# A routing step handed out earlier, and the last group of a gated layer in another order

## The chip, the core and the metric

The program runs on one core of one Trainium2 chip. The core has five engines with instruction streams of their own: TensorE (PE, matmuls and transposes through the array; its weight loads are listed as PEld), VectorE (DVE), ScalarE (ACT), GpSimd (POOL) and SyncE (SP, which only issues DMAs and loads of registers). They wait for each other by semaphores. The metric is the time of one execution on the device, in microseconds; less is better. For before, the median of three runs is 842.74 us (839.76 to 843.46).

## The reference

Three layers follow each other on 2304 tokens of 512 numbers, all in float32:

```python
# 1: attention over a feature map, 4 batches x 8 heads x 576 positions
phi(x) = concat(exp(p), exp(-p)),  p = x @ w_phi - max|x @ w_phi|
attn   = (phi(q) @ (phi(k)^T v)) / (phi(q) @ sum phi(k))

# 2: mixture of 8 experts, each token goes to one of them
logits = x @ w_gate + modality_bias[modality_id]
e_idx  = argmax(logits);  gate_w = softmax(logits)[e_idx]
out[t] = gate_w[t] * (relu(x[t] @ w1[e_idx]) @ w2[e_idx])      # 512 -> 1024 -> 512

# 3: gated layer
result = ((x @ w_a) * (x @ w_b)) @ w_out                       # 512 -> 1536 -> 512
```

## The kernel before

Matrices are multiplied to float32 accuracy with three matmuls each: both factors are split into a high part and a remainder, and `mm3` (L53 to L56) adds high x high (L54), high x low (L55) and low x high (L56). The remainders are made by DVE (`wl` L553, `mxl` L577, `hl` L591, `gl` L829).

**Halves, tiles and steps.** The tokens are taken in two halves of 1152, each with a routing of its own (`Route`). A routing has four parts: `start` (gate and one-hot), `rank` (a matmul `rkp`, copied to `R` at L394), `place` (sorts the tokens to tiles of up to 608 tokens of one expert; writes `meta`, L464) and `table` (two matmul lookups: `tbp` gives `idx`, the tokens of each tile in order, L504; `tbq` gives the places `perm` and gates `g` of the output, L504 and L514 to L517). Its matmuls use PSUM tiles of the pool `ps_t`, which has two buffers under one tag; the transposes of the tiles use the same two.

Each half has two tiles, so there are T0, T1 (first half) and T2, T3 (second half). `Moe.run` goes through them in 8 steps a tile, step k = 8 x tile + j. Steps j = 0 to 3 are the first matrix (`l1`, 48 matmuls `hp` each), steps 4 to 7 the second (`l2`, 48 matmuls `yp` each). For the tile that comes next, the gathers (`gather`, five of them, an indirect DMA on POOL's queue by `idx`, L561, into `xg`) are asked for at j = 2, and the transposes (`transp`, five pieces of four PE transposes into `mxt`, L573, then ACT's high part `mxh` and DVE's remainder `mxl`) at j = 4 to 7. Pieces 0 to 2 hold the 304 tokens with which the first `hp` of a tile work.

**Work beside.** The dictionary `side` hands out other work at a step: the four parts of the second half's routing, `close_work` (L945 of before: the largest tile count `top` of both halves), and ten conversions of the gated layer's weights from 64-bit numbers, as they come, to float32 (`conv`, with `prep` and `narrow`: loads `raw` on SP's queue L685, ACT L689, POOL L690, DVE L691 to L698, sums L707 to L710, split L715 and L716, stores L717 and L718). All of these are handed out with a lower priority (`low`, LOWR; `conv`, LOWP).

**Who sets the order.** In this stage a scheduler sets the order of every engine's instructions before the program runs: it goes by priority and by its own estimate of when operands are ready. Each engine then runs its list strictly in order. So a part handed out at another step moves many instructions on many engines.

**The gated layer.** `Moe2.run` goes through 24 groups (token blocks of 768, each taken through 12 blocks of 128 of the 1536 hidden columns). In a group `stage` has seven input products (`PROD`, six matmuls `abp` each; a scheme with seven products in place of eight), from which ACT and DVE build the gated values `gh`, `gl`. The output products `outp(k, m)` (three matmuls `op`) add a group to six accumulators m. Before, outp of the group before stands between the input products, and the last group's six outp stand at the very end (L873 to L875). When an accumulator is complete, `finish` scales it (ACT for even m, DVE for odd) and stores it by an indirect DMA on POOL's queue (L797). PE's order is the order of the code here (`manual_schedule`).

Of the kernel before, what the change touches and what calls it, by code (L numbers as in the profile page):

```python
# [48 lines left out]
def f32(ap):  # L49
    return ap.bitcast(F32)  # L50
# [604 lines left out]
class Moe2:  # L655
# [124 lines left out]
    def run(self, ws, ts, src0, side):  # L780
        nc, n = self.nc, self.N
        seq = [(p, f) for p in range(NTOK // n // 2) for f in range(self.NF)]
        accs, gs = {}, {}

        def finish(p):
            for m, acc in enumerate(accs.pop(p)):
                bp, b = divmod(2 * p + m // 3, HALF // n)
                if m % 3 == 0:
                    os = self.p_o.tile([P, 3, DM], F32, tag="raw", name="o", bufs=2)
                o = os[:, m % 3, :]  # L790
                c = b * (n // P) + m % 3
                g2 = self.routes[bp].g2[:, c:c + 1]
                if m % 2:
                    nc.vector.tensor_scalar(out=o, in0=acc, scalar1=g2, scalar2=None, op0=ALU.mult)
                else:
                    nc.scalar.activation(o, acc, AF.Copy, scale=g2)  # L796
                st = nc.gpsimd.indirect_dma_start(  # L797
                    out=self.out[:, :],
                    out_offset=bass.IndirectOffsetOnAxis(ap=self.routes[bp].perm[:, c:c + 1], axis=0),
                    in_=o, in_offset=None)  # L800
                for other in self.stores:
                    self.tc.declare_no_dep(st.ins, other, reason="each row of the output is stored once")
                self.stores.append(st.ins)

        def outp(k, m):
            p, f = seq[k]
            if f == 0 and m == 0:
                accs[p] = [self.ps_a.tile([P, 512], F32, tag=f"a{i}", name=f"op{i}") for i in range(6)]
            gh, gl = gs[k]
            wh, wl = ws[k](1536, 512)  # L810
            ms = slice(P * (m % 3), P * (m % 3) + P)
            mm3(nc, accs[p][m], gh[:, m // 3, ms], gl[:, m // 3, ms], wh, wl, f == 0, f == self.NF - 1)
            if m == 5:
                del gs[k], ws[k]
                if f == self.NF - 1:
                    finish(p)

        def stage(k):
            p, f = seq[k]
            ct = lambda tag, shape: self.p_c.tile([P] + shape, F32, tag=tag, name=tag)  # L820
            ca, u, d = ct("ca", [2, n]), ct("u", [2, n]), ct("d", [2, n])
            out = []
            gs[k] = [self.p_g.tile([P, 2, n], F32R, tag=t, name=t) for t in ("gh", "gl")]

            def gate(i, other):
                gh, gl = (x[:, i, :] for x in gs[k])
                nc.vector.tensor_mul(ca[:, i, :], ca[:, i, :], other)  # L827
                nc.scalar.copy(gh, ca[:, i, :])  # L828
                nc.vector.tensor_sub(gl, ca[:, i, :], f32(gh))  # L829

            for i, (col, t) in enumerate(self.PROD):
                ps = self.ps_l.tile([P, 512], F32, tag="l", name="abp")[:, :n]
                wh, wl = ws[k](col, 256)
                th, tl = ts[p][t]
                for c in range(2):
                    cs = slice(P * c, P * c + P)
                    mm3(nc, ps, wh[:, cs], wl[:, cs], th[:, c, :], tl[:, c, :], c == 0, c == 1)
                x = self.p_c.tile([P, n], F32, tag="pc", name="pc", bufs=5)
                nc.scalar.copy(x, ps)  # L839
                out.append(x)  # L840
                if i == 1:
                    nc.vector.tensor_add(u[:, 0, :], x, out[0])
                elif i == 2:
                    nc.vector.tensor_add(ca[:, 0, :], x, out[0])
                elif i == 3:
                    nc.vector.tensor_add(u[:, 1, :], x, u[:, 0, :])
                elif i == 4:
                    nc.vector.tensor_add(d, u, x.unsqueeze(1).to_broadcast([P, 2, n]))  # L848
                elif i == 5:
                    nc.vector.tensor_add(x, x, u[:, 1, :])  # L850
                    gate(0, x)
                elif i == 6:
                    nc.vector.tensor_add(ca[:, 1, :], x, d[:, 0, :])
                    gate(1, d[:, 1, :])
                if k and i > 1:
                    for m in (i - 2,) if i < 6 else (4, 5):
                        outp(k - 1, m)

        src = src0
        self.rest(src, ts[0])  # L860
        for k, (p, f) in enumerate(seq):
            with self.tc.high_priority(offset=-LOWP2):
                for st in side.get(k, ()):
                    st()
            if k + 1 < len(seq) and k + 1 not in ws:
                ws[k + 1] = self.weights(k + 1)
            if f == 0 and p:
                self.rest(src, ts[p])
            with self.tc.manual_schedule(engines={mybir.EngineType.PE}):
                stage(k)  # L870
            if f == self.NF - 2 and k + 2 < len(seq):
                src, ts[p + 1] = self.terms(p + 1, self.p_s)
        with self.tc.manual_schedule(engines={mybir.EngineType.PE}):  # L873
            for m in range(6):
                outp(len(seq) - 1, m)  # L875


def low(tc, step):
# [8 lines left out]
def trn_kernel(ctx, tc, qk, v, vt, w_phi, mod_id, w_gate, bias, wm, wf, out):  # L887
# [37 lines left out]
    with ExitStack() as mctx:  # L925
        ps_t = mctx.enter_context(tc.tile_pool(name="ps_t", bufs=2, space=PSUM, **tl))
        ps_l = mctx.enter_context(tc.tile_pool(name="ps_l", bufs=3, space=PSUM, **tl))
        ypool = ctx.enter_context(tc.tile_pool(name="y", bufs=1, **tl))
        y = [ypool.tile([P, 4, YC], F32, name=f"y{i}") for i in range(2)]
        m2 = Moe2(nc, tc, wf, wsc, y, routes, out, f64)  # L930
        mo = Moe(nc, tc, mctx, cst, xs, wm, y, ps_l, ps_t)
        tiles = [(rt, t) for rt in routes for t in range(NTMIN)]
        rctx = ExitStack()
        cv = []
        nts = []
        ws = {}

        cctx = ExitStack()
        cv.append(cctx.enter_context(tc.tile_pool(name="cv", bufs=1, **tl)))

        def close_work():
            rctx.close()
            top = rpool.tile([1, 1], I32, name="top")
            n = slice(3 * NTMAX, 3 * NTMAX + 1)
            nc.vector.tensor_tensor(out=top, in0=routes[0].meta[:, n], in1=routes[1].meta[:, n], op=ALU.max)  # L945
            nts.append(nc.values_load(top[:, :], min_val=0, max_val=NTMAX))

        wk1 = rctx.enter_context(tc.tile_pool(name="rwork1", bufs=1, **tl))
        rs = routes[1].steps(wk1, ps_t, "t")
        side = {k: [low(tc, rs[f])] for f, k in enumerate((0, 3, 5, 8))}  # L950
        side[9] = [close_work]

        def conv(f):
            with tc.high_priority(offset=-LOWP):
                m2.prep(f, cv[0], 2, 2)

        K0, K1 = 3, len(tiles) * mo.NJ - 4
        for f in range(NPRE):
            side.setdefault(K0 + (K1 - K0) * f // NPRE, []).append(lambda f=f: conv(f))
        ts, src0 = {}, []  # L960

        def first():
            src, ts[0] = m2.terms(0, m2.p_s, ts.get(0), src0[0] if src0 else None)
            src0.append(src)

        def open_first():
            cctx.close()
            m2.p_t[0] = ctx.enter_context(tc.tile_pool(name="f_t", bufs=Moe2.NT0, **tl))
            m2.p_s = ctx.enter_context(tc.tile_pool(name="f_s", bufs=1, **tl))
            m2.p_w[0] = ctx.enter_context(tc.tile_pool(name="f_w0", bufs=1, **tl))  # L970
            ws[0] = m2.weights(0)
            with tc.high_priority(offset=-LOWP):
                first()

        side.setdefault(K1, []).append(open_first)
        tc.mark_branch_hint_location("extra", "LikelyTaken", engines=ENGINES)
        mo.run(tiles, side)
        with tc.If(nts[0] > NTMIN, label="extra"):
            n = slice(3 * NTMAX, 3 * NTMAX + 1)
            for rt in routes:  # L980
                extra(tc, mo, rt, nc.values_load(rt.meta[:, n], min_val=0, max_val=NTMAX))
            first()
    cv.append(ctx.enter_context(tc.tile_pool(name="cv2", bufs=1, **tl)))
    side = {}
# [65 lines left out]
```

## Time and profile before

| what | before |
|---|---|
| runs, us | 842.74, 843.46, 839.76 |
| profiled execution, us | 840.43 |
| its span, us | 838.6 |
| PE busy, us | 802.0 |
| DVE busy, us | 595.5 |
| POOL busy, us | 134.1 |

The profiled execution's span is what the profile covers; the little that lies around it makes the difference to 840.43. A row of a timeline begins with the start of an instruction in the span, then its duration, its engine, its line in the kernel and what it writes and reads. Matmuls are pipelined, so the distance of two starts, and not the duration, is what one costs. Where an engine was idle before an instruction, square brackets give the time and what ended it.

### The profile page before, as it was taken

The numbers are of one execution on the slowest core, as the hardware profiler recorded it, in microseconds if no ns is written. First come the engines' busy times: TensorE is split into PE (matmuls) and PEld (weight loads), VectorE is DVE, ScalarE is ACT, GpSimd is POOL, SyncE is SP. The second block draws the span as 40 slices with busy tenths as digits, with TensorE's granted clock in tenths as the row PEclk, the third lists the DMA queues.
The fourth block names the chain that finished last, engine by engine and source line by source line (L and its number), as shares of the span: only waits on it lengthen the run. The fifth ranks groups of instructions, "written<-read, shape, count | busy, mean of one in ns | idle before, by whom it ended". The sixth has DMA issues, their size and how long they took to land.

```text
span 838.6 us, 18331 instructions
## 1 busy us (share of the span) xinstructions
PE 802.0 (96%) x7284; PEld 752.8 (90%) x7284; DVE 595.5 (71%) x1071; ACT 375.1 (45%) x665; POOL 134.1 (16%) x164
## 2 busy tenths in 40 slices
PE   9999998899989999989899999999999999999995
PEld 7989888899989999989889899989999999999994
DVE  6877998689995989797588855675554476545553
ACT  4555555434452555444445433553333364333332
POOL 1000018433233522510031000020000002000002
PEclk9999999999998999999999999999999999999998
DMA  8755431667668888776689876576666668666631
GB/s 300 221 173 165 161 90 31 215 217 275 225 202 283 295 303 295 239 288 251 230 286 332 280 241 201 195 257 214 225 202 199 192 201 301 202 203 201 190 135 75
DMA packets 85163, 184.22 MB, mean 220 GB/s; under 512 B 27760, under 2 KB 37520, under 8 KB 85072
## 3 DMA queue, kind: packets, MB, share of 16 engines
q1 hardware_dynamic: 81872, 173.21, 61.6%
q0 software_dynamic: 3040, 9.72, 3.2%
q8 instruction: 58, 0.95, 0.5%
q14 instruction: 33, 0.27, 0.1%
q10 hardware_dynamic: 160, 0.07, 0.0%
HBM read 145.21 MB, written 37.75 MB: 218 GB/s over the span
## 4 chain that ended last, share of the span: by engine, by line
PE 24%; issue 19%; DVE 4%; POOL 2%; ACT 2%; DMA 1%; POOLq 0%; DVEq 0%; ACTq 0%
PE abp L54 5%; PE abp L56 5%; PE abp L55 5%; PE op L56 3%; PE op L55 3%; PE op L54 3%; POOL cvs L690 1%; DMA wsc<-whi 1%; POOL out L797 1%; ACT pc L839 1%; DVE gl L829 0%; DVE d L848 0%; ACT yh L744 0%; DVE ca L827 0%; DVE yl L745 0%
## 5 line engine op out<-in xcount | busy, mean ns | idle before, releaser
L839 ACT COPY pc<-abp 128x384 f32<-128x384 f32 x252 | 120.5, 479 | 199.3 <-PE abp L56 194.2
L54 PE MATMUL abp<-yh,fw 128*128 128x384 f32 x504 | 169.9, 337 | 3.2 <-ACT pc L839 2.2
L55 PE MATMUL abp<-yl,fw 128*128 128x384 f32 x504 | 169.9, 337 | 0.0
L56 PE MATMUL abp<-yh,fw 128*128 128x384 f32 x504 | 169.9, 337 | 0.0
L54 PEld LDWEIGHTS abp<-yh,fw 128*128 128x128 f32 x504 | 94.6, 188 | 13.1 <-ACT pc L839 4.0
L55 PEld LDWEIGHTS abp<-yl,fw 128*128 128x128 f32 x504 | 94.6, 188 | 7.6
L690 POOL TENSOR_SCALAR cvs<-cvs 128x768 f32<-128x768 f32 x24 | 62.7, 2612 | 210.5 <-ACT cvs L689 158.3
L56 PEld LDWEIGHTS abp<-yh,fw 128*128 128x128 f32 x504 | 94.6, 188 | 0.0
L54 PE MATMUL op<-fw,gh 128*128 128x512 f32 x216 | 85.4, 395 | 1.0 <-ACT gh L828 1.0
L56 PE MATMUL op<-fw,gl 128*128 128x512 f32 x216 | 85.3, 395 | 0.9 <-DVE gl L829 0.9
L55 PE MATMUL op<-fw,gh 128*128 128x512 f32 x216 | 85.4, 395 | 0.0
L54 PE MATMUL hp<-mxh,wh 128*128 128x304 f32 x256 | 78.8, 309 | 3.7 <-DVE hl L591 3.7
L55 PE MATMUL yp<-hl,wh 128*128 128x304 f32 x256 | 77.1, 302 | 1.0 <-DVE hl L591 1.0
L55 PE MATMUL hp<-mxl,wh 128*128 128x304 f32 x256 | 77.9, 305 | 0.0
L56 PE MATMUL yp<-hh,wl 128*128 128x304 f32 x256 | 77.7, 304 | 0.0
L56 PE MATMUL hp<-mxh,wl 128*128 128x304 f32 x256 | 77.7, 304 | 0.0
L54 PE MATMUL yp<-hh,wh 128*128 128x304 f32 x256 | 76.7, 303 | 0.5 <-ACT y L603 0.5
L797 POOL DMA_INDIRECT out<-o,perm x18 | 18.1, 1006 | 355.9 <-ACT o L796 349.4
L190 ACT ACTIVATE qts<-qtp 128x512 f32<-128x512 f32 (+1 forms) x80 | 38.3, 557 | 57.2 <-PE qtp L187 57.2
L848 DVE TENSOR_TENSOR d<-u,pc 128x768 f32<-128x768 f32 x36 | 34.4, 956 | 33.9 <-ACT pc L839 33.7
L54 PEld LDWEIGHTS hp<-mxh,wh 128*128 128x128 f32 x256 | 48.7, 191 | 4.9 <-DVE hl L591 2.8
L828 ACT CAST gh<-ca 128x384 fp32r<-128x384 f32 x72 | 36.9, 515 | 34.6 <-DVE ca L827 34.6
(191 smaller groups left out, 1584.4 us busy)
## 6 DMA issues: line engine op xcount, KB each, us to landing
fw<-wsc SPq DMA_DIRECT2D x72, 512.0 KB, 3.6
fw<-wsc SPq DMA_DIRECT2D x144, 256.0 KB, 3.3
raw<-in_moe_w SPq DMA_DIRECT2D x24, 768.0 KB, 6.2
s<-in_moe_w SPq DMA_DIRECT2D x32, 512.0 KB, 5.8
fw<-wsc SPq DMA_DIRECT2D x72, 128.0 KB, 2.6
wsc<-whi SPq DMA_DIRECT2D x12, 640.0 KB, 4.8
wsc<-wsum SPq DMA_DIRECT2D x12, 640.0 KB, 5.0
wsc<-whi SPq DMA_DIRECT2D x12, 512.0 KB, 4.2
```

The costliest lines, as they stand in the source:

```text
L54: nc.tensor.matmul(out, lh, rh, start=start, stop=False)
L55: nc.tensor.matmul(out, lh, rl, start=False, stop=False)
L56: nc.tensor.matmul(out, ll, rh, start=False, stop=stop)
L190: nc.scalar.activation(t[:, s, :n, :], ps[:, :n, :], AF.Exp, scale=1.0 - 2.0 * s)
L690: nc.gpsimd.tensor_scalar(out=s.bitcast(F32), in0=s.bitcast(F32), scalar1=LEAST, scalar2=None, op0=ALU.max)
L797: st = nc.gpsimd.indirect_dma_start(out=self.out[:, :], out_offset=bass.IndirectOffsetOnAxis(ap=self.routes[bp].perm[:, c:c + 1], axis=0), ...
L828: nc.scalar.copy(gh, ca[:, i, :])
L839: nc.scalar.copy(x, ps)
L848: nc.vector.tensor_add(d, u, x.unsqueeze(1).to_broadcast([P, 2, n]))
```

## The change

Two things. The parts of the second half's routing are handed out at steps 0, 1, 2 and 4 (all within T0) instead of 0, 3, 5 and 8. And in the last of the 24 groups of the gated layer all seven input products come first, in the order 0, 1, 2, 3, 5, 4, 6; behind them stand the output products of the group before (back 1) and of the last one (back 0), accumulator by accumulator.

```diff
-            for i, (col, t) in enumerate(self.PROD):
+            last = k + 1 == len(seq)
+            for i in (0, 1, 2, 3, 5, 4, 6) if last else range(7):
+                col, t = self.PROD[i]
...
-                if k and i > 1:
+                if k and i > 1 and not last:
                     for m in (i - 2,) if i < 6 else (4, 5):
                         outp(k - 1, m)
...
                 stage(k)
+                if k + 1 == len(seq):
+                    for back, m in ((1, 0), (1, 1), (1, 2), (0, 0), (0, 1), (0, 2), (1, 3), (0, 3), (1, 4), (0, 4), (1, 5), (0, 5)):
+                        outp(k - back, m)
...
-        with self.tc.manual_schedule(engines={mybir.EngineType.PE}):
-            for m in range(6):
-                outp(len(seq) - 1, m)
...
-        side = {k: [low(tc, rs[f])] for f, k in enumerate((0, 3, 5, 8))}
+        side = {k: [low(tc, rs[f])] for f, k in enumerate((0, 1, 2, 4))}
         side[9] = [close_work]
```

The first change moves instructions on all engines from the mixture's first steps on. On PE, in the order of before, T1's transposes stand among the `yp` of T0's last steps; these are the rows around the last of its five pieces (96 tokens wide):

```order
L54 MATMUL yp<-hh,wh 128x304
L55 MATMUL yp<-hl,wh 128x304
L573 MATMUL mxt<-ident,xg 128x96 x4
L56 MATMUL yp<-hh,wl 128x304
L54 MATMUL yp<-hh,wh 128x304 x2
L55 MATMUL yp<-hl,wh 128x304
```

Behind them T0 goes on. In the order of after, no transposes of T1 are left there: the whole five pieces stand behind the last `yp` of T0, with the second half's lookup `tbq` (`tbqr` and `lhs` are its operands, made by DVE) between them:

```order
L56 MATMUL yp<-hh,wl 128x304
L497 LDWEIGHTS lhs
L497 MATMUL tbq<-tbqr,lhs 128x45
L573 MATMUL mxt<-ident,xg 128x128 x4
...
L497 LDWEIGHTS lhs
L497 MATMUL tbq<-tbqr,lhs 128x45
L573 MATMUL mxt<-ident,xg 128x128 x12
L54 MATMUL hp<-mxh,wh 128x304 x3
L573 MATMUL mxt<-ident,xg 128x96 x4
L55 MATMUL hp<-mxl,wh 128x304
```

In the rows left out stand seven more `tbq`. In the order of before the `tbq` stand inside T1's second half of steps, directly ahead of the first transposes of T2.

On DVE, in the order of after, this stands from the last `tbqr` to the first `mxl` of T1 (`cvs`, `cvt`, `wsum` are tiles of the weight conversions, `wl` the remainder of an expert's weights):

```order
L493 TENSOR_TENSOR tbqr<-tbqh,gp 128x9x9 x3
L695 TENSOR_SCALAR cvs<-cvt 128x768
L947 TENSOR_TENSOR top<-meta_2204,meta_3445 1x1
L698 TENSOR_TENSOR wsum<-cvt,cvs 128x768
L553 TENSOR_TENSOR wl<-s,wh 128x1024
L716 TENSOR_TENSOR wsum<-wsum,whi 128x1280
L553 TENSOR_TENSOR wl<-s,wh 128x1024
L696 SCALAR_TENSOR_TENSOR cvs<-raw,cvs 128x768
L503 TENSOR_SCALAR tk<-tbq 128x9
L577 TENSOR_TENSOR mxl<-mxt,mxh 128x4x128
```

The second `mxl` comes eight rows further, the third nine rows after that, the fourth and fifth two rows after each one before. Between them stand further conversions (L691, L693, L695 to L698, L707 to L710) and the small steps of `perm` and `g`.

In the gated layer's last group, PE's rows in the order of after run on from the seven products like this (the name `op_16900` is accumulator 0; rows on an accumulator come in threes):

```order
L56 MATMUL abp<-yh,fw 128x384
L54 MATMUL op_16900<-fw,gh 128x512
L55 MATMUL op_16900<-fw,gh 128x512
L56 MATMUL op_16900<-fw,gl 128x512
L54 MATMUL op_16901<-fw,gh 128x512
...
L54 MATMUL op_16902<-fw,gh 128x512
L55 MATMUL op_16902<-fw,gh 128x512
L56 MATMUL op_16902<-fw,gl 128x512
L54 MATMUL op_16900<-fw,gh 128x512
L55 MATMUL op_16900<-fw,gh 128x512
L56 MATMUL op_16900<-fw,gl 128x512
```

The first three accumulators get the group before, then the last group, and after them come 3, 4 and 5, each with both groups one behind the other. In before, the last group's products stood between the accumulations of the group before, and accumulators 0 to 5 of the last group at the end.

## Rows read from the trace of the kernel before

**Rows 1.** The page's first part: an engine's busy time, share of span, instructions.

```profile
PE 802.0 (96%) x7284; PEld 752.8 (90%) x7284; DVE 595.5 (71%) x1071; ACT 375.1 (45%) x665; POOL 134.1 (16%) x164
```

**Rows 2.** Waits of PE, whole run: us in total, times, longest.

```profile
PE mxt L573 <- DMA xg<-xs,idx: 5.2, 1, 5.2
PE hp L54 <- DVE hl L591: 3.7, 5, 1.1
```

**Rows 3.** Busy by stretch: length, PE, PEld, DVE, ACT, POOL, clock, DMA share, GB/s.

```profile
205.00:245.00 40.00, 40.00 (x297) 39.73 (x297) 39.92 (x95) 18.72 (x29) 9.86 (x4) 1.00 0.66 220
```

**Rows 4.** Timeline of PE where T2's transposes stand: start, us, what.

```profile
247.75 0.40 PE L497 MATMUL tbq<-tbqr,lhs 128*128 128x45 bf16 x9
253.37 1.09 PE L573 MATMUL mxt<-ident,xg 128*128 128x128 f32 x4 [5.22 <-DMA xg<-xs,idx]
257.30 0.31 PE L54 MATMUL hp<-mxh,wh 128*128 128x304 f32 x1
```

**Rows 5.** Busy by stretch, the 2 us behind that wait; clock third last.

```profile
252.00:254.00 2.00, 0.63 (x3) 0.66 (x4) 2.00 (x6) 0.00 (x0) 1.59 (x2) 0.50 0.95 311
```

**Rows 6.** Timeline of PE at the end of T0 and start of T1.

```profile
215.31 0.60 PE L573 MATMUL mxt<-ident,xg 128*128 128x128 f32 x4
...
215.89 0.30 PE L55 MATMUL yp<-hl,wh 128*128 128x304 f32 x1
...
223.66 0.30 PE L54 MATMUL hp<-mxh,wh 128*128 128x304 f32 x1
...
224.91 0.30 PE L54 MATMUL hp<-mxh,wh 128*128 128x304 f32 x1
```

**Rows 7.** Timeline of DVE: an `hl`, the second routing's `R`, its last `tbqr`.

```profile
187.95 0.77 DVE L591 SCALAR_TENSOR_TENSOR hl<-hp,hh 128x608 fp32r<-128x608 f32 x1
...
205.04 0.23 DVE L394 COPY R<-rkp 128x80 f32<-128x80 f32 x1
...
244.17 0.53 DVE L493 TENSOR_TENSOR tbqr<-tbqh,gp 128x81 bf16<-128x81 bf16 x3
```

**Rows 8.** DVE by line and shape, 185 to 248: busy, mean ns, idle before.

```profile
L553 DVE TENSOR_TENSOR wl<-s,wh 128x1024 fp32r<-128x1024 f32 x9 | 11.3, 1252 | 0.0
...
L696 DVE SCALAR_TENSOR_TENSOR cvs<-raw,cvs 128x768 f32<-128x768 uint32 x6 | 5.7, 946 | 0.0
...
L691 DVE TENSOR_SCALAR cvt<-cvs 128x768 int32<-128x768 int32 x6 | 3.3, 550 | 0.3 <-POOL cvs L690 0.3
...
L716 DVE TENSOR_TENSOR wsum<-wsum,whi 128x1280 fp32r<-128x1280 f32 x2 | 3.0, 1479 | 0.0
L577 DVE TENSOR_TENSOR mxl<-mxt,mxh 128x512 fp32r<-128x512 f32 x4 | 2.7, 677 | 0.0
L716 DVE TENSOR_TENSOR wsum<-wsum,whi 128x1024 fp32r<-128x1024 f32 x2 | 2.4, 1214 | 0.0
...
L708 DVE TENSOR_TENSOR wsum<-wsum 128x256 f32<-128x256 f32 x3 | 1.2, 415 | 0.0
```

**Rows 9.** Timeline of POOL and DVE beside one conversion's maximum.

```profile
212.97 3.44 POOL L690 TENSOR_SCALAR cvs<-cvs 128x768 f32<-128x768 f32 x1 [5.15 <-ACT cvs L689]
...
213.13 0.95 DVE L696 SCALAR_TENSOR_TENSOR cvs<-raw,cvs 128x768 f32<-128x768 uint32 x1
214.00 0.42 DVE L710 TENSOR_TENSOR wsum<-wsum 128x256 f32<-128x256 f32 x1
...
214.60 1.58 DVE L553 TENSOR_TENSOR wl<-s,wh 128x1024 fp32r<-128x1024 f32 x1
```

**Rows 10.** Timeline of PE and POOL at the end of the run.

```profile
827.00 0.97 POOL L797 DMA_INDIRECT out<-o,perm  x1 [126.31 <-ACT o L796]
...
828.49 0.39 PE L55 MATMUL op<-fw,gh 128*128 128x512 f32 x1
...
828.72 0.39 PE L56 MATMUL op<-fw,gl 128*128 128x512 f32 x1
...
833.37 0.97 POOL L797 DMA_INDIRECT out<-o,perm  x1 [0.30 <-issue]
```

## The prediction

> **What bounds the kernel now.** I read the page's engine line first: PE is busy for 802.0 of 838.6 us [rows 1], so the order of PE's work is the kernel, and only what makes PE wait can be won or lost. Second the waits of PE over the run [rows 2]: 5.2 us in one piece at the transposes `mxt`, waiting for the gather `xg`, and 3.7 us in five pieces at `hp`, waiting for `hl` from DVE. Third the busy time by stretch around the second routing [rows 3]: from 205 to 245 us PE is busy for 40.00 of 40 us, and so is DVE, for 39.92, with 95 instructions. PE has no gap there only because DVE keeps just ahead of it. That is what matters most: work that DVE must do for PE there and that is put behind other DVE work costs PE time at once.
>
> Fourth PE's timeline where the third tile (T2, first of the second half) begins [rows 4]. After the last `tbq` of the second routing PE stands 5.22 us for the gather, and 4 transposes with the first 12 `hp` then take from 253.37 to 257.30, 3.93 us. In that stretch the granted clock is 0.50 [rows 5], the lower of its two levels (1.2 of 2.4 GHz), after PE had been nearly idle. At full clock the same work is taken from [rows 6]: 4 transposes and the `yp` behind them take 0.58 (215.31 to 215.89), so 0.44 for the transposes; nine `hp` take 1.25 (223.66 to 224.91), 0.139 each, so twelve 1.67. That makes 2.11, and the slow clock cost 1.82.
>
> The profiled execution took 840.43 us. The sum is made against it; the median of the three runs, 842.74, lies 2.3 higher, and the predicted time is the median plus the sum.
>
> **What the earlier routing removes.** The second half's `idx` is made in T0's last step instead of T1's third, so the gathers of T2 are issued a tile ahead of the transposes that need them: the 5.22 goes, and the 1.82 with it. -7.0. What is late next is what the rest of this text is about.
>
> **What it adds: T1's start.** In the order of before, T1's transposes stand among the last `yp` of T0, each with PE work behind it [rows 6]. In the order of after, the routing's `tbp` and `tbq` take the two PSUM buffers that the transposes share with it, and all five pieces of T1 stand behind T0's last `yp`: one `tbq`, 4 transposes, eight `tbq`, 12 transposes, then the `hp` that need them. The pieces take turns in two buffers, so a piece waits for the DVE subtraction `mxl` of an earlier one (the third for the last L516, which reads `tbq`), and the first `hp` waits for the third `mxl`. DVE's order therefore decides. Between its last `tbqr` and that third `mxl` stand 26 instructions, mostly weight conversions. With the means of [rows 8], 0.15 for each of the small ones (the 0.23 of `R` [rows 7] is the longest of these), L693 and L698 taken as L696 (same shape, two inputs), L695 as L691, L707 and L709 as L708, and 0.08 off each for overlap (213.13 + 0.95 against the next start at 214.00 [rows 9]):
> - to the first `mxl`: 0.55 + 0.946 + 1.252 + 1.479 + 1.252 + 0.946 + 0.677 and two small ones, less 0.72: 6.7
> - to the second: 0.55 + 0.946 + 0.946 + 0.415 + 0.677 and three small ones, less 0.64: 3.3
> - to the third: 0.55 + 3 x 0.415 + 2 x 0.946 + 0.677 and two small ones, less 0.72: 3.9
>
> Together 14.0 us from the last `tbqr` to the first `hp`. The fourth and fifth `mxl` are 1.7 and 0.9 later, and the 12 `hp` of the first token group cover them. PE's own work in the stretch at full clock is 0.40 for `tbq` [rows 4], 5 x 0.44 for transposes and 1.67 for 12 `hp`: 4.3. If the clock falls as in [rows 5], the twelve `hp` and the fifth piece take 3.9 behind the 14.0: 17.9, a loss of 13.6. If it doesn't fall, the loss is 14.0 less the 1.7 of `tbq` and three pieces: 12.3.
>
> To this comes PE's wait for `tbqr` itself. `R`, from the second routing's rank, stands in the order of after right behind the `hl` that began at 187.95 [rows 7], so at about 188.7 instead of 205.04. From `R` to the end of `tbqr` DVE needed 39.7 us (205.04 to 244.70), for 93 instructions that come to 39.5 by the means above; in the order of after there are 88, without the four `mxl` and one `wl`, and they come to 36.6, 2.9 less. 188.7 + 36.8: `tbqr` ends near 225.5. PE gets there at 223.66 plus 24 `yp` that still followed (3.3) less five pieces (2.2), some 224.7. Wait 0.8, between 0 and 3. The term is 13.6 + 0.8 = +14.4, from 12.3 (no clock loss, no wait) to 18 (a raw block for the conversions comes late as well).
>
> **The rest of T1.** DVE owes T1's `hl` in time: 42 instructions stand between its last `mxl` and the eighth, by the same means ([rows 8], with the 0.77 of [rows 7] for an `hl`) 30.5 us, so 47.1 from `tbqr`. PE wants it after the 17.9, 180 more `hp` (25.0), two pieces of T2 (0.9) and 21 `yp` (2.9): 46.7. +0.5, 0 to 3. The other waits for `hl`, 3.7 [rows 2], may go or grow with any shift: -1.0 taken, for DVE has four `mxl` less in T0's last steps; -3.7 to +3 as bounds.
>
> **The last gated group.** In the order of after all seven products stand first and then, for the first accumulator, the output product of the group before and of the last. Nine matmuls (accumulators 3 to 5 of the group before) no longer stand ahead of the first finished accumulator: 9 x 0.23 ([rows 10], 828.49 to 828.72) is 2.1. The six stores run on GpSimd 1.27 apart, 827.00 to 833.37, and set the end; starting 2.1 sooner, the last starts at 831.3. The last accumulator is still done in time, since the last matmul stays at 828.72, 2.6 before that. -2.1, from -1 (ACT's casts of the gate lie ahead of the first scaling) to -2.6. Order 5 before 4 costs nothing: the same seven products.
>
> Sum: +14.4 + 0.5 - 7.0 - 1.0 - 2.1 = +4.8, which is 845.2 against the profiled execution and **847.5** against the median.
>
> **Rivals.** What this measurement can tell from no change is about 0.5%, 4.2 us: 838.5 to 847.0 counts as the same.
>
> A, faster: DVE is well ahead of PE at T1's start and PE stands under 5 us. For it: `tbqr` needs only `R` and fixed work, and PE may be later than reckoned. Against: DVE would have to be 9 us earlier, and in 205 to 245 it has 0.08 us idle [rows 3]. With a stand of 2.5: 2.5 - 7.0 - 1.0 - 2.1 = -7.6, so 835.1.
>
> B, no change: T1's stand is at its low end and the waits for `hl` go: 12.3 - 7.0 - 3.7 - 2.1 = -0.5, so 842.2. For it: a PE that stands lets DVE catch up. Against: the order of DVE in T1 is as full as before.
>
> C, slower still: GpSimd's maximum L690 comes late. Its input comes by SP's queue, and in the order of after SP waits for the second half's `meta` earlier, with a weight and a raw load behind it; then DVE's L691 in the second leg waits for one L690, up to 3.44 [rows 9]. Against: in before DVE waited 0.3 for it in this whole stretch [rows 8]. 847.5 + 3.4 = 850.9.
>
> D, slower still: DVE and GpSimd shut each other out. The chain's L696 and L698 have two SBUF inputs, and GpSimd runs two L690 beside it in the order of after; DVE would stand up to 3.44 for each, 847.5 + 6.9 = 854.4. While L690 ran from 212.97 to 216.41, DVE's L696 took 0.95, its mean, and L553 1.58 against 1.252, and L690 itself was the slow one [rows 8, 9]: at most 0.33 is seen. The Trainium skill (SBUF — State Buffer, Who interferes with whom) states the strict form: a DVE instruction with two SBUF inputs contends with a GpSimd instruction that reads SBUF, and the later one blocks fully until the other ends. By that rule the time would be D's; the trace doesn't bear it out, since L696 ran inside an L690 without a loss.
>
> **How the numbers follow.** Forecast 0.45, its own range 844.5 to 851.5 (T1's term from 12.3 to 18, the others near their values), 0.30 of it above 847.0 and 0.15 below. B 0.26, all within 0.5%. A 0.13. C 0.11 and D 0.05, slower. So slower 0.46, same 0.41, faster 0.13. The range 839.5 to 854 leaves out most of A and a part of D and of late loads.
>
> **What would show it.** PE's waits after: the 5.2 for `xg` gone, and 12 to 14 us at `mxt` and `hp` for `mxl`, right after T0's last `yp`, in three pieces near 6, 3 and 4, with a granted clock of 0.50 behind them. The first store near 2 us sooner against the last product. I am wrong if PE's stand there is under 9 us, if a wait of over 3 us appears at another place, or if gathers of T2 are still waited for.

## The result, and the profile after

The changed kernel takes 850.8 us (median of six runs, 847.28 to 851.18) against 840.23 for before on the same chip: a ratio of 1.0125, 95% interval 1.0100 to 1.0151. It is slower, by 10.6 us. The forecast was slower by 4.8 (847.5 us, range 839.5 to 854): side and mechanism held, the size was less than half of what came. That the time itself lies only 3.3 above the forecast is partly luck: before's median was 842.74 when the forecast was made and is 840.23 over all six runs.

Four slips in the text ahead: the gated layer goes through 36 groups (three blocks of 768 tokens), not 24; `tbq` of before stands among T1's `hp`, not in its second half of steps; T2's gathers now begin 27 us ahead of its first transposes (227.77 and 255.07), not a whole tile; and three `hp` by L54, which need no `mxl`, stand ahead of the third `mxl`, as the rows of the order show, so the first `hp` doesn't wait for it. The first three bear on no number of the sum; by the fourth the stand was put some 0.8 us too long.

The profiled execution of after took 851.02 us with a span of 849.2. First the engine line of its page, then the waits of PE from 200 to 300 us (total, times, longest):

```profile
PE 806.3 (95%) x7283; PEld 754.6 (89%) x7284; DVE 596.8 (70%) x1071; ACT 375.9 (44%) x665; POOL 138.3 (16%) x164
```

```profile
PE mxt L573 <- issue: 5.7, 1, 5.7
PE mxt L573 <- DVE mxl L577: 5.7, 2, 4.8
PE hp L54 <- DVE hl L591: 1.2, 1, 1.2
PE yp L54 <- ACT hh L590: 0.9, 1, 0.9
PE yp L55 <- DVE hl L591: 0.6, 1, 0.6
PE tbq L497 <- DVE tbqr L493: 0.6, 1, 0.6
```

The 5.2 for the gather [rows 2] is gone. In its place stand 5.7 and 5.7 at T1's transposes. PE's timeline there:

```profile
226.76 0.18 PE L497 MATMUL tbq<-tbqr,lhs 128*128 128x45 bf16 x1 [0.58 <-DVE tbqr L493]
...
233.43 1.09 PE L573 MATMUL mxt<-ident,xg 128*128 128x128 f32 x4 [5.74 <-issue]
239.28 2.32 PE L573 MATMUL mxt<-ident,xg 128*128 128x128 f32 x8 [4.77 <-DVE mxl L577]
...
243.25 0.90 PE L573 MATMUL mxt<-ident,xg 96*128 96x96 f32 x4 [0.89 <-DVE mxl L577]
...
247.27 0.30 PE L54 MATMUL hp<-mxh,wh 128*128 128x304 f32 x1
```

The wait that the profile calls "issue" ends at 233.43, right after the first `mxl` (232.66 + 0.67): it is a wait for DVE as well. The first matmul that runs at full pace again stands at 247.27. Busy time by stretch (length, PE, PEld, DVE, ACT, POOL, clock, DMA share, GB/s) shows the granted clock, the third last number, falling to 0.50 once PE has stood, as in [rows 5], and back at 1.00 only after 247 us:

```profile
228.00:230.00 2.00, 0.00 (x0) 0.00 (x0) 2.00 (x3) 1.02 (x2) 2.00 (x1) 1.00 0.96 395
230.00:232.00 2.00, 0.00 (x0) 0.00 (x0) 2.00 (x3) 0.00 (x0) 2.00 (x1) 0.54 0.91 274
...
244.00:246.00 2.00, 2.00 (x9) 2.00 (x9) 2.00 (x5) 0.48 (x1) 1.66 (x2) 0.50 0.93 278
...
248.00:250.00 2.00, 2.00 (x16) 2.00 (x16) 0.56 (x2) 1.27 (x1) 2.00 (x1) 1.00 0.99 404
```

DVE's timeline, the first three `mxl` and the one place where DVE itself stands:

```profile
232.66 0.67 DVE L577 TENSOR_TENSOR mxl<-mxt,mxh 128x512 fp32r<-128x512 f32 x1
235.78 0.56 DVE L691 TENSOR_SCALAR cvt<-cvs 128x768 int32<-128x768 int32 x1 [2.45 <-POOL cvs L690]
...
238.55 0.68 DVE L577 TENSOR_TENSOR mxl<-mxt,mxh 128x512 fp32r<-128x512 f32 x1
...
242.51 0.68 DVE L577 TENSOR_TENSOR mxl<-mxt,mxh 128x512 fp32r<-128x512 f32 x1
```

And GpSimd, for which DVE waits 2.45 us there:

```profile
227.77 5.80 POOL L561 DMA_INDIRECT xg<-xs,idx  x1 [9.30 <-PE tbq L497]
233.59 2.15 POOL L690 TENSOR_SCALAR cvs<-cvs 128x768 f32<-128x768 f32 x1
```

One gather of T2 sits on GpSimd for 5.80 us (the shortest of this trace take 0.91), and the maximum L690 for the conversion is queued behind it. The end of the run, against [rows 10], from the first product of the last group to the first and the last of the six stores; the last row is the same product in before:

```profile
826.25 0.33 PE L54 MATMUL abp<-yh,fw 128*128 128x384 f32 x1
...
837.59 0.97 POOL L797 DMA_INDIRECT out<-o,perm  x1 [123.86 <-ACT o L796]
...
843.96 0.97 POOL L797 DMA_INDIRECT out<-o,perm  x1 [0.30 <-issue]
...
813.22 0.33 PE L54 MATMUL abp<-yh,fw 128*128 128x384 f32 x1
```

From product to first store it is 11.34 us; before it was 13.78 (813.22 to 827.00): 2.4 sooner.

Read at the same places of PE's work, the two profiled executions part like this (start in the span, us):

| place | before | after | after later by |
|---|---|---|---|
| first `hp` of T0 | 169.23 | 169.47 | 0.2 |
| first `yp` of T1 | 262.32 | 274.13 | 11.8 |
| 97th `yp` of T2 | 334.25 | 349.39 | 15.1 |
| 97th `yp` of T3 | 391.48 | 404.47 | 13.0 |
| last store | 833.37 | 843.96 | 10.6 |

So T1 costs 11.8, T2 some 3.3 more, T3 gives 2.1 back and the last group 2.4.

### The profile page after: what moved, and what is told of

Same layout as the page of the kernel before. It is cut to its first block, busy times and chain, and to the rows that moved or that the text cites. A ratio compares the mean times of both kernels' runs of the same rounds, so it can differ in the third digit from the quotient of the medians.

```text
span 849.2 us, 18329 instructions
## 1 busy us (share of the span) xinstructions
PE 806.3 (95%) x7283; PEld 754.6 (89%) x7284; DVE 596.8 (70%) x1071; ACT 375.9 (44%) x665; POOL 138.3 (16%) x164
## 4 chain that ended last, share of the span: by engine, by line
PE 27%; issue 16%; DVE 4%; ACT 1%; POOL 1%; DMA 1%; POOLq 0%; SPq 0%; ACTq 0%; DVEq 0%
PE abp L54 6%; PE abp L56 6%; PE abp L55 6%; PE op L56 3%; PE op L55 3%; PE op L54 3%; DMA wsc<-whi 1%; ACT pc L841 0%; POOL cvs L690 0%; DVE gl L829 0%; POOL out L797 0%; ACT yh L744 0%; DVE ca L827 0%; DVE d L850 0%; DVE cvt L693 0%
## 5 line engine op out<-in xcount | busy, mean ns | idle before, releaser
L54 PE MATMUL abp<-yh,fw 128*128 128x384 f32 x504 | 170.1, 337 | 3.0 <-ACT pc L841 2.0
L54 PEld LDWEIGHTS abp<-yh,fw 128*128 128x128 f32 x504 | 94.6, 188 | 13.0 <-ACT pc L841 4.0
L690 POOL TENSOR_SCALAR cvs<-cvs 128x768 f32<-128x768 f32 x24 | 58.5, 2438 | 201.9 <-ACT cvs L689 201.8
L54 PE MATMUL op<-fw,gh 128*128 128x512 f32 x216 | 85.4, 395 | 1.0 <-ACT gh L828 1.0
L54 PE MATMUL hp<-mxh,wh 128*128 128x304 f32 x256 | 78.9, 310 | 3.7 <-DVE hl L591 3.7
L54 PE MATMUL yp<-hh,wh 128*128 128x304 f32 x256 | 77.5, 304 | 2.1 <-ACT y L603 1.1
L553 DVE TENSOR_TENSOR wl<-s,wh 128x1024 fp32r<-128x1024 f32 x32 | 39.6, 1236 | 21.8 <-ACT wh L552 21.8
L54 PEld LDWEIGHTS hp<-mxh,wh 128*128 128x128 f32 x256 | 48.9, 192 | 4.6 <-issue 3.5
```

The lines of the kernel that those rows point to most:

```text
L54: nc.tensor.matmul(out, lh, rh, start=start, stop=False)
L553: nc.vector.tensor_sub(lo, src, f32(hi))
L690: nc.gpsimd.tensor_scalar(out=s.bitcast(F32), in0=s.bitcast(F32), scalar1=LEAST, scalar2=None, op0=ALU.max)
```

## The experiments

The theory after the result: T1's five transposes are handed out behind the two lookups, so they get the two shared PSUM buffers after them, and DVE, which works through its list of conversions without a pause, comes late to each `mxl` that frees a buffer. Rivals: the buffers' order alone; DVE's load alone; and, for the part that was not forecast, GpSimd.

The ratios below, with their 95% intervals, are to before on the same chip and lie up to 0.2% off the quotient of the medians; the chips differ from one group of runs to the next. In the twelve profiled executions the first `hp` of T0 stands anywhere between 168.0 and 174.4 us, for which no cause is shown, so traces are compared by lengths from there on. "The mixture" is from that `hp` to the last `yp` of T3: 236.2 us in before, 249.2 in after.

**e1 and e2: the two edits apart.**

```text
e1:  side = {... enumerate((0, 1, 2, 4))}, last group as before
e2:  side = {... enumerate((0, 3, 5, 8))}, last group as after
```

> The routing steps of after with the last gated group of before. Theory: the last group is worth -2.1 us by itself, so this kernel is 2.1 slower than after, about 853 against 840.2 for before, with PE's stand of some 12 us at T1's start unchanged. Rival: the new last group gains nothing (the stores are bound by something else): same as after, 850.8.

> The routing steps of before with the last gated group of after. Theory: -2.1 us, about 838 against 840.2, the first of the last six stores 2.1 sooner against the last group's first product. Rival: 0, because the stores' order is set elsewhere.

e1: 858.45 against 843.61, ratio 1.0156 (1.0114 to 1.0199): +14.8 by the medians, +13.2 by the ratio. The stand is the one of after, to the hundredth, and the first gather of T2 takes 5.80 again:

```profile
239.24 1.08 PE L573 MATMUL mxt<-ident,xg 128*128 128x128 f32 x4 [5.74 <-issue]
245.10 2.32 PE L573 MATMUL mxt<-ident,xg 128*128 128x128 f32 x8 [4.77 <-DVE mxl L577]
249.07 0.90 PE L573 MATMUL mxt<-ident,xg 96*128 96x96 f32 x4 [0.89 <-DVE mxl L577]
```

e2: 841.35, ratio 0.9970 (0.9935 to 1.0004), -2.3, with 1.0 just inside the interval. The loss belongs to the routing steps. What the last group gains is clearer in the traces than in the times: from its first product to the first store it takes 13.8 us in before and in e1, which have the old order, and 11.34 to 11.45 in after and in the nine other runs, which have the new one.

**e3: the table behind T1's transposes.**

```diff
-        side = {k: [low(tc, rs[f])] for f, k in enumerate((0, 1, 2, 4))}
+        side = {k: [low(tc, rs[f])] for f, k in enumerate((0, 1, 2, 8))}
```

> Routing parts at steps 0, 1, 2 and 8 in place of 0, 1, 2 and 4, the last group as in after. All five transposes of T1 are now handed out before the table's two lookups, so they take the shared PSUM buffers first and stand inside T0 again. Theory (the buffers' order costs the stand): PE's waits for mxl at T1's start fall from 12 us to about 2, the wait for the gather of T2 from 5.2 in before to 1 at most, and the time is about 834 (840.2 - 2.1 for the last group, -7 for T2's gather, +2 to 3 for T1). Rival (DVE is overloaded there whatever the order of the buffers): the stand moves to another wait for DVE and the time is 840 or more.

836.9 us, ratio 0.9907 (0.9872 to 0.9941): faster than before, and by its ratio than after (1.0125). The mixture takes 232.6 us, 3.6 less than in before. PE's waits from 200 to 300 us:

```profile
PE hp L54 <- ACT y L603: 1.7, 2, 1.0
PE yp L55 <- DVE hl L591: 0.8, 1, 0.8
PE hp L54 <- DVE g L515: 0.7, 1, 0.7
PE hp L54 <- DVE hl L591: 0.6, 1, 0.6
```

No wait for `mxl`, and none for the gather of T2. `idx` is written 65.9 us behind the first `hp` of T0, in before 74.8, and T1's transposes go through without a wait, four pieces in T0 and the fifth among T1's first `hp`. This is the version that beats both kernels.

**e4: the lookups in other PSUM buffers.**

```diff
-        rs = routes[1].steps(wk1, ps_t, "t")
+        rs = routes[1].steps(wk1, ps_l, "l")
```

> After, with the second routing's three PSUM tiles taken from the pool of hp and yp (three buffers) and no longer from the two buffers of the transposes. The order of the engines then has T1's transposes in T0, but puts the lookup tbp ahead of T0's first yp. Theory (DVE reaches the routing's steps far later than the order assumes): from R to tbpr DVE has 33 us of work by the durations in the trace, PE comes 20 us after R's matmul, so the stand moves to tbp, about 12 us there, none at T1's start, none for T2's gather: about 844. Rival (the shared buffers alone make the stand): no wait over 3 us, about 831.

869.14, ratio 1.0293 (1.0232 to 1.0353): 25 us slower, where 4 was expected. Three of PE's stands:

```profile
212.35 1.11 PE L573 MATMUL mxt<-ident,xg 128*128 128x128 f32 x4 [5.80 <-DVE mxl L577]
...
228.40 0.20 PE L497 MATMUL tbq<-tbqr,lhs 128*128 128x45 bf16 x1 [7.04 <-DVE tbqr L493]
...
257.78 0.59 PE L54 MATMUL yp<-hh,wh 128*128 128x304 f32 x1 [8.48 <-DVE g L516]
```

The rival as stated falls: with the lookups out of the two buffers, PE still waits for `mxl` at T1's transposes. But the run doesn't part the buffers from DVE's load, since the lookups now share three buffers with `hp` and `yp`, and the third stand comes from that. Each stand is for DVE, since the order of the engines puts T1's transposes and the lookups where DVE is not yet done; the stand expected at `tbp` was 1.5 us instead of 12, and the long ones came at `mxt` and `tbq`. The third was in no expectation. GpSimd and DVE ahead of it:

```profile
226.72 6.95 POOL L561 DMA_INDIRECT xg<-xs,idx  x1 [4.27 <-DVE wsum L707]
...
237.75 0.92 POOL L561 DMA_INDIRECT xg<-xs,idx  x1 [0.30 <-issue]
238.69 4.25 POOL L690 TENSOR_SCALAR cvs<-cvs 128x768 f32<-128x768 f32 x2
...
240.88 2.48 DVE L691 TENSOR_SCALAR cvt<-cvs 128x768 int32<-128x768 int32 x1 [8.12 <-POOL cvs L690]
```

All five gathers of T2 stand ahead of L690, the first takes 6.95, DVE stands 8.12 us in the middle of its list, and L516 (which frees `tbq`'s buffer for `yp`) is behind that.

**e5: halfway.** Steps 0, 1, 2 and 6.

> Routing parts at steps 0, 1, 2 and 6, the last group as in after: the halfway house between after (table at 4) and e3 (table at 8). Three of T1's five transposes are handed out ahead of the lookups and two behind. Theory (whoever is handed out first has the shared buffers, and DVE reaches the later ones late): the first 36 hp of T1 go on, then PE stands for the last two mxl, which by the durations of DVE's list come 48.7 us after R, some 7 us after PE wants them: a stand of 6 to 9 us, the time between e3 and after, about equal to before (ratio 0.995 to 1.005). Rival (it is the lookups' own lateness that counts, not the transposes' place): as after, 1.01 or more.

840.36 against 844.79, ratio 0.9959 (0.9933 to 0.9986). The time came as expected, between e3 and after. The stand is shorter than expected, 3.0 us in four waits in T1 (0.32, 1.20, 0.57, 0.95) besides 1.46 for `y` at its first `hp`, where e3 has 1.01, and the granted clock is still 1.00 up to 242 us. With the table at 4, 6 and 8 the ratios are 1.0125, 0.9959 and 0.9907, each to before on its own chip.

**e6 and e7: a lighter DVE.** The same edit, which leaves out the low words of the weights, on the steps of after (e6) and of before (e7), both with the last group of after:

```diff
-        nc.vector.scalar_tensor_tensor(out=t, in0=hi, ...
+        nc.vector.scalar_tensor_tensor(out=dst.bitcast(I32), in0=hi, ...
...
-        nc.vector.tensor_scalar(out=s, in0=t, scalar1=-0x800000, ...
-        nc.vector.scalar_tensor_tensor(out=s.bitcast(F32), in0=lo..., ...
-        nc.vector.tensor_add(dst, t.bitcast(F32), s.bitcast(F32))
```

> After, with the weight conversions made lighter for DVE: the low words of the gated layer's weights are left out (three of DVE's five operations of 128x768 in each conversion go; the two that stay are 1.5 us in place of 3.9). Theory (T1's stand is DVE's queue of conversions between tbqr and the mxl): the third mxl comes 43.6 us after R in place of 50.9 by the durations, the stand falls from 12 to about 5 us, and against e7 (the same without low words, old steps) the early routing costs 2 to 6 us, where it cost 13 at the full load. Rival (the PSUM buffers' order alone makes the stand): it costs 10 or more here too.

> The partner of e6: the same lighter conversions (low words left out), routing parts at steps 0, 3, 5 and 8, the last group as in after. Theory: about 832 on a chip where before has 842, since PE's waits for hl shrink and T2's transposes stand later; both theories expect no stand over 3 us at T1's start.

e6: ratio 0.9964 (0.9940 to 0.9989); e7: 0.9916 (0.9894 to 0.9939). The difference of the medians is 3.6 us, where the early routing costs 13 at the full load (e1). PE's waits for `mxl` at T1's transposes in e6, 200 to 300 us:

```profile
PE mxt L573 <- DVE mxl L577: 4.1, 2, 3.5
```

So the stand goes with DVE's load, as the theory says; the order of buffers says for whom PE stands, DVE's queue says how long. Some of it may be GpSimd's part: two of the three operations left out have two inputs in SBUF, no gather of e6 takes over 1.71 us, and DVE doesn't wait for L690 in this stretch. (e7 was expected at 832 on a chip with 842 for before, a ratio of 0.988; it came at 0.992.)

**e8: e3 with one conversion fewer beside the mixture.** `NPRE` 9 in place of 10.

> e3 with nine conversions instead of ten beside the mixture, the tenth beside the gated layer, whose DVE is half idle. The order of the mixture's start is that of e3. If DVE's load still costs something in T2 and T3 (waits for hl of 2.7 us and for y of 1.7 in e3), 1 to 3 us less than e3, about 0.988 of before; if the conversion collides with the gated layer's start, as much more.

838.8, ratio 0.9926 (0.9900 to 0.9953): no gain over e3. The mixture takes 232.5 us, as long as in e3 (232.6): PE's waits for `hl` at `hp` fall from 2.7 to 1.5, those for `y` rise. The gated layer up to its last group takes 410.2 against 406.4, which fits the collision that was expected there. One conversion less buys nothing; whether a much lighter DVE would, the run doesn't show.

**e9 and e10: who holds up whom.**

```diff
-        nc.gpsimd.tensor_scalar(out=s.bitcast(F32), in0=s.bitcast(F32), scalar1=LEAST, scalar2=None, op0=ALU.max)
+        nc.gpsimd.memset(s.bitcast(F32), LEAST)
```

> After, with GpSimd's maximum over the high words (L690, which reads and writes SBUF) replaced by a fill of the same tile with a constant (it only writes); the weights' magnitudes are left out by that. The same DVE and ACT steps wait for it. Theory (a GpSimd instruction that reads SBUF is held up while DVE runs an instruction with two SBUF inputs, and this is what cost DVE 2.45 us in after): the fills all take the same time to within 0.2 us whatever DVE does beside them, the gathers, which read idx, are still stretched in places, DVE doesn't wait for L690 between tbqr and the third mxl, and that stretch takes 13.4 us by the durations of DVE's list, where it took 16.5 in after; so 2 to 3 us less than after, ratio to before about 1.009. Rival (the stretching is the profile's rough spans on GpSimd): the fills vary as L690 did, and the time is that of after.

> The kernel after, unchanged, for comparison with e9 on one chip: 1.0125 of before, 16.5 us from the last tbqr to the third mxl, and the first gather of T2 stretched to 5.8 us again if that is no accident of one run.

e9: 846.75 against 838.64, ratio 1.0096 (1.0064 to 1.0127). e10: 851.57, ratio 1.0145 (1.0102 to 1.0188), with the gather of 5.80 and DVE's wait of 2.45 again. e9 is 4.8 us below e10 by the medians, where 2 to 3 was expected. GpSimd from 168 to 400 us, by line and shape (count, busy, mean ns, idle before), of e9 and of e10:

```profile
L561 POOL DMA_INDIRECT xg<-xs,idx x11 | 16.6, 1510 | 23.7 <-PE mxt L573 22.5 <-issue 1.2
L690 POOL MEMSET cvs<- 128x768 f32 x20 | 14.9, 743 | 122.6 <-ACT cvs L689 122.6
```

```profile
L690 POOL TENSOR_SCALAR cvs<-cvs 128x768 f32<-128x768 f32 x20 | 49.0, 2451 | 96.3 <-ACT cvs L689 96.2
L561 POOL DMA_INDIRECT xg<-xs,idx x13 | 25.1, 1928 | 20.8 <-PE mxt L573 9.3 <-DMA raw<-in_moe_w 9.3 <-issue 1.9
```

The twenty fills took 0.74 to 0.76 each, whatever DVE did beside them; the maximum took 2.13 to 3.65 in e10. A fill is also a shorter instruction, but three fills lay whole inside an instruction of DVE with two inputs in SBUF that had begun before them, and they took no longer than the four beside which DVE did nothing:

```profile
221.39 1.21 DVE L716 TENSOR_TENSOR wsum<-wsum,whi 128x1024 fp32r<-128x1024 f32 x1
...
221.75 0.74 POOL L690 MEMSET cvs<- 128x768 f32 x1 [5.81 <-ACT cvs L689]
```

The gathers are still stretched in e9 (two of 2.99 and 3.13). The time of e9 says less. The scheduler sets another order there: an L691 stands at 225.69, ahead of the first `mxl`, with the last fill done at 222.49, and none stands in the second leg, where it waited in after. That DVE doesn't wait for L690 between `tbqr` and the third `mxl` therefore follows from the order already. That stretch took 15.1 us (224.63 to 239.77) in place of 16.5, since DVE now waited 1.77 for ACT's `mxh` instead; without it 13.4, as expected. And the 4.8 is a sum of larger parts: in the profiled executions the mixture takes 242.0 us in e9 and 249.4 in e10, the gated layer up to its last group 413.2 and 405.5. So the 4.8 is no measure of the hold.

## Why the prediction was right, and where its size was off

**T1's start, forecast +14.4.** The mechanism came as written: stands for DVE in three pieces, at the places named. By the profile PE was ready for `tbq` at 226.18 (226.76 less 0.58) and started its 13th `hp` of T1 at 246.28: 20.1 us, of which 4.3 are its own work at full clock, so 15.8 lost, 1.4 more than forecast. DVE reached the end of `tbqr` at 226.7 (forecast 225.5); the legs to the three `mxl` were 6.6, 5.9 and 4.0, where 6.7, 3.3 and 3.9 had been added up. Two legs are right to 0.1. The mis-sized one is the second, and its surplus is the 2.45 that DVE waited for L690. PE lost less than that on top, because the three `hp` that need no `mxl` ran ahead of the third.

**That wait is rivals C and D in one.** C had DVE waiting for L690 in exactly this leg, but by a late `raw`. D had the two engines shutting each other out, priced on DVE's side, and was put aside because L696 had run beside an L690 at its usual length. The row that spoke for D was in the same group: the L690 of 3.44 [rows 9] was not slow by itself, it was the one held up. Of its kind the shortest take 2.12. So that L696 lost nothing beside it doesn't speak against D's rule, as the prediction had it: there GpSimd was the one shut out. The step that failed was to look only at what DVE loses: GpSimd's delay counts too once DVE waits for GpSimd.

Other rows of before show the hold without any change. Where L690 begins inside an unbroken run of DVE instructions with two inputs in SBUF, and DVE then stands, it ends a fixed time behind that run:

```profile
334.82 4.24 POOL L690 TENSOR_SCALAR cvs<-cvs 128x768 f32<-128x768 f32 x1 [8.34 <-ACT cvs L689]
...
335.86 1.21 DVE L553 TENSOR_TENSOR wl<-s,wh 128x1024 fp32r<-128x1024 f32 x1
339.10 0.56 DVE L691 TENSOR_SCALAR cvt<-cvs 128x768 int32<-128x768 int32 x1 [2.02 <-POOL cvs L690]
```

L553 ends at 337.07, L690 at 339.06, 1.99 later. The eleven traces that have the maximum hold 31 such L690, begun at least 0.3 before the end of the run. Of these 23, between 2.40 and 4.88 us long, end 1.98 to 1.99 behind it. The other eight get in sooner, and in each it is an instruction of DVE's run that is longer than usual, like L710 in after at 298.58 (1.58 in place of 0.41). So one of the two is held, and which one differs. Spans that were merely rough would not do that.

In after, the gather of 5.80 ran beside five DVE instructions with two inputs in SBUF, one behind the other, and ended 1.0 after DVE had gone on to L503 (232.58), which reads PSUM; in e9, behind a shorter run, the gather of 2.99 ended 0.9 after the start of L503 there. The Trainium skill (SBUF — State Buffer, Who interferes with whom) states that such an instruction contends with a GpSimd one that reads SBUF, not with one that only writes it, and that the later one blocks fully; e9's fills, the L690 above and these gathers agree with it. They don't settle all of it: a gather of before, from 250.50 to 251.80, ran beside two such DVE instructions (L553 and L716) and took 1.30. When GpSimd gets in between two of them stays open.

**T2's gather, forecast -7.0.** Right: the wait is gone in after, e1 and e3.

**The rest of the mixture, forecast +0.5 and -1.0.** The +0.5 for T1's `hl` came as one wait of 1.2 at 267.37, at an `hp`. It goes back to a late load, which the prediction had among its bounds for T1's start: ACT's L689 waited for `raw`, the cast L552 stood behind it, DVE waited for that cast, and the `hl` at 266.44 stands two rows further on DVE.

```profile
262.56 0.89 ACT L689 ACTIVATE cvs<-raw 128x768 f32<-128x768 f32 x1 [3.05 <-DMA raw<-in_moe_w]
...
264.43 1.23 DVE L553 TENSOR_TENSOR wl<-s,wh 128x1024 fp32r<-128x1024 f32 x1 [1.84 <-ACT wh L552]
```

The -1.0 was wrong in sign. PE's waits for `hl` and `hh` between the second and third place of the table are 4.0 us against 1.1 in before, which is most of T2's 3.3; between the third and fourth all its waits are 0.4 against 2.6, which is T3's 2.1. The reason given, four `mxl` less in T0, shows in T0 alone, where the wait for `hl` falls from 0.99 to 0.65. Why T2 loses and T3 gains stays open.

**The last group, forecast -2.1.** Measured -2.4 in the profile, and the same in all twelve traces (13.8 with the old order, 11.3 to 11.5 with the new one). By the times it is not clear of nothing: e2 against before is -2.3 with 1.0 inside the interval, and the intervals of after and e1 overlap.

So the sum: the profiled executions differ by 10.6 in span, 5.8 more than forecast. T1 has 3.9 of it: 1.4 in the stand, 0.4 for four further `hp` at the low clock, 0.7 by which the wait at 267.37 exceeds the 0.5 put there, 0.2 a later start of T0, and 1.2 not accounted for, in which some 0.4 is a second piece of T2's transposes that stands ahead of T1's first `yp` in after and behind it in before. The later tiles have 2.2, and the last group takes 0.3 back.

**What the forecast had not asked** is whether the early routing could be had without its price. Its use is T2's gather; its price is that the table is handed out ahead of T1's transposes. e3 keeps the one without the other, at the cost of one number.

## What to carry to other kernels

Where a planner sets the order and two jobs share a small ring of buffers, the order of handing out can decide who waits: here the lookups had the lower priority and still got the buffers first. Look for what is handed out just ahead of the work that the bounding engine needs next. Then add up the waited-for engine's own list in the planned order, with durations from the trace; an engine that was full in the stretch is the place where an order that looks free on paper isn't. And an instruction that varies in length while its shape doesn't is a row to follow: what it waits for, and who waits for it.

## What the hardware showed that was not expected

GpSimd's indirect gather took between 0.91 and 6.95 us, and its 128x768 maximum between 2.12 and 6.25; both lengths go with DVE's instructions beside them, the maximum's to the hundredth in the 23 places named above. It also goes the other way, for an L710 of 1.58 above. And in e3, as in e8, a DVE step with one SBUF input, which usually takes 0.55, took 2.92 while GpSimd ran L690:

```profile
247.10 2.92 DVE L695 TENSOR_SCALAR cvs<-cvt 128x768 int32<-128x768 int32 x1
...
247.44 2.15 POOL L690 TENSOR_SCALAR cvs<-cvs 128x768 f32<-128x768 f32 x1
```

It ended 0.43 after L690 did. That L690 held it is argued from these two rows, not tested.
